# Eleven stretches of an attention kernel in another written order, and rows spread by GpSimd instead of by loads

## The chip, the cores and the metric

The kernel runs on one core of a Trainium2 chip. The metric is the device time of one execution in microseconds (us). A core has five engines that run at the same time, each through its own queue in the order in which its instructions are written: TensorE (PE; its weight loads are listed as PEld), VectorE (DVE), ScalarE (ACT), GpSimd (POOL) and SyncE (SP). SyncE only issues DMAs here: loads, and transposes of bf16 tiles. ScalarE and GpSimd issue a few DMAs too. All of them share 16 DMA engines.

## What is computed

Two blocks over the same 2048 rows of 640 numbers, multiplied at the end. Block A is attention of the normalized rows over the last 512 keys of a cache, 32 heads of 192, one key head for each query head. Block B picks the two rows with the largest dot product with a vector w_r, sends them through a gated feed-forward layer, and adds the result to those rows.

```
xn = layernorm(x)
q  = (xn @ wq) in 32 heads of 192
s  = softmax(q k^T / sqrt(192)) v, joined, @ wo        # k, v: last 512 of the cache
r  = xn @ w_r;  idx = the 2 rows with the largest r
y  = (silu(xn[idx] @ w_gate) * (xn[idx] @ w_up)) @ w_down * sigmoid(r[idx])
g  = silu(xn + y scattered to rows idx)
out = x + s * g
```

## The kernel before

**Tiling.** Rows lie in 16 blocks of 128. Heads come in pairs, and four heads make a group (8 groups). A *step* is one pair of heads for 512 rows; a *unit* is one pair for 128 rows, so there are 64 steps and 256 units. Units go through the engines in *stretches*: two of 2 units, then 84 of 3.

**A unit's way.** The letters are the tokens in which the order is written.

- `q.i.c` (L301): five matmuls project 512 rows for 128 of step i's 384 columns; `qe.i.c` scales the result out of PSUM on ScalarE (`a`) or VectorE (`v`), L291 and L293. With a row range at its end, a token is for half the rows; those evacuations go to ScalarE whatever their letter.
- `S.j` (L315, L322): scores of all units of a stretch, two PSUM tiles for a unit.
- `M.n.h` (L330): row maximum on VectorE. `E.n.h` (L337): exponential and row sum on ScalarE.
- `P.n` (L342): SyncE issues the DMA transpose of the exponentials.
- `O.n`, `OO.n.m` (L356): eight matmuls with v. `R.j` (L346) inverts the row sums; `Oe.n` (L371 or L369) scales the result on VectorE or ScalarE; `T.j` (L377) transposes a stretch's results by DMA.
- `W.w` (L404): twelve matmuls with wo for 128 rows and one group of heads; `We.w` copies or adds them into s_acc (L416, L418).

**Normalizing** stands at the front, among the first stretches. `bn` (L163, L165) takes statistics on VectorE, `as` (L233 to L235) by two ScalarE passes and a small GpSimd operation. 1 / deviation comes by `sq` and `rc` (square root on ScalarE, reciprocal on VectorE) or by `pw`, four GpSimd operations with a power of -0.5 (L211 to L214). `ap` (L249, L251) applies it. Blocks 0 to 3 are transposed by TensorE (`turn`, L258, L259), the others by DMA (`xT`, L262). The first k tile is transposed by TensorE too (`kt`, L273, L274).

**Loads**: `x`, `k`, `v`, `wq`, `wo` on SyncE, or on ScalarE with an `a` at the end; `kT` (L119) transposes a k tile by DMA. `B` tokens stand for work of block B, of which the first eleven stretches have none.

**Buffers.** PSUM has two tiles of kind f (q, and o of the `O` token) and six of kind p (scores, w, and o of `OO`). The exponentials have four buffers (`p_pool`), their transposes six, transposed q three.

**What sets the order.** The kernel turns Tile's scheduling off: each engine runs its instructions exactly as the tokens are written. The first eleven stretches, S.0 to S.10, are written by hand in the string FIRST; from S.11 on `stretch(j)` writes the same pattern each time, with projections and output projections dealt out by a small plan (2 or 3 `q`, 1 or 2 `W` a stretch); the last stretches are by hand again (LAST).

**Block B** runs beside it. `m_open` loads w_r to all partitions (L444). `m_top` finds candidates in each block and sends them through DRAM to all partitions (L489, L491), `m_sel` reads them (L497). `m_down` sends the feed-forward's two rows through DRAM to all partitions (L612, L614), and `m_add` adds them on GpSimd to the chosen rows (L618 to L622).

Of the kernel before, what the change touches and what calls it, by code (L numbers as in the profile page):

```python
# [12 lines left out]
FP32 = mybir.dt.float32  # L13
BF16 = mybir.dt.bfloat16
# [7 lines left out]
def kernel(ctx, tc, A_x, A_k_cache, A_v_cache, A_wq, A_wo, B_x, B_w_r, B_w_gate, B_w_up, B_w_down, out):  # L22
    nc = tc.nc
    P = 128
    _, S, D = A_x.shape
# [49 lines left out]
    def f_tile(shape, dtype, name):  # L75
        return ps_f.tile(shape, dtype, name=name, tag="f")
# [60 lines left out]
    for _ in range(10):  # L137
# [5 lines left out]
        out=ident_f, in_=ident_f, compare_op=ALU.not_equal, fill=1.0, base=0,  # L143
# [291 lines left out]
    M = {}  # L435

    def m_open():
        late.close()
        M["stack"] = ExitStack()
        M["w"] = M["stack"].enter_context(tc.tile_pool(name="moe_w", bufs=1))  # L440
        M["s"] = M["stack"].enter_context(tc.tile_pool(name="moe_s", bufs=1))
        M["ws"] = (M["w"], M["s"])
        M["wr"] = M["s"].tile([P, D], BF16, name="wr_bc", tag="t3")
        nc.gpsimd.dma_start(out=M["wr"], in_=B_w_r.partition_broadcast(P))  # L444
        M["r"] = M["s"].tile([P, NTB], FP32, name="r_pn")
        M["r_b"] = M["s"].tile([P, P], BF16, name="r_b", tag="turned")
# [12 lines left out]
        nc.gpsimd.iota(M["cpos"], pattern=[[1, NCD]], base=0, channel_multiplier=0, allow_small_or_imprecise_dtypes=True)
# [16 lines left out]
    def m_top():  # L476

        rows = M["s"].tile([NTB, P], FP32, name="r_rows", tag="rows")
        nc.vector.tensor_copy(out=rows, in_=M["rT"][0:NTB, :])
        top = M["s"].tile([NTB, 8], FP32, name="top8")  # L480
        loc = M["s"].tile([NTB, 8], U32, name="loc8")
        nc.vector.max(out=top, in_=rows)
        nc.vector.max_index(out=loc, in_max=top, in_values=rows)
        cand = M["s"].tile([NTB, 2, 2], FP32, name="cand")
        nc.vector.tensor_copy(out=cand[:, 0, :], in_=top[:, 0:2])
        nc.vector.tensor_copy(out=cand[:, 1, :], in_=loc[:, 0:2])
        nc.vector.tensor_scalar(out=cand[:, 1, :], in0=cand[:, 1, :], scalar1=M["base"][:, 0:1], scalar2=None, op0=ALU.add)  # L487
        c_d = tc.dram_tile([NTB, 2, 2], FP32, name="c_d")
        nc.gpsimd.dma_start(out=c_d, in_=cand)  # L489
        M["cand"] = M["w"].tile([P, NTB, 2, 2], FP32, name="cand_bc", tag="w")  # L490
        nc.gpsimd.dma_start(out=M["cand"].rearrange("p n k c -> p (n k c)"), in_=c_d.rearrange("n k c -> (n k c)").partition_broadcast(P))  # L491
# [108 lines left out]
    DQ = D // 4  # L600

    def m_down():
        y_ps = f_tile([P, DQ], FP32, "y_ps")
        for fc in range(FC):
            for c in range(4):
                nc.tensor.matmul(y_ps[32 * c:32 * c + 32], lhsT=M["hT"][:, fc, :], rhs=M["wd"][:, fc, c * DQ:(c + 1) * DQ],
                                 start=(fc == 0), stop=(fc == FC - 1), skip_group_check=True)
        y_sb = M["s"].tile([P, DQ], BF16, name="y_sb", tag="t2")
        nc.vector.tensor_scalar(out=y_sb, in0=y_ps, scalar1=M["sgp"][:, 0:1], scalar2=None, op0=ALU.mult)  # L609
        y_d = tc.dram_tile([2, D], BF16, name="y_d")  # L610
        for c in range(4):
            nc.gpsimd.dma_start(out=y_d[:, c * DQ:(c + 1) * DQ], in_=y_sb[32 * c:32 * c + 2, :])  # L612
        M["y_bc"] = M["w"].tile([P, 2, D], BF16, name="y_bc", tag="w")
        nc.gpsimd.dma_start(out=M["y_bc"], in_=y_d.partition_broadcast(P))  # L614

    def m_add(n):
        def f():
# [162 lines left out]
    for j in range(2, NST):  # L780
        due = sum(st_of[4 * i] <= j + 1 for i, _ in todo)
        k = max(due, 2) if j % 4 != 1 else max(due, 3)
# [3 lines left out]
        k = 2 if len(ready) >= 2 and len(q_in[j]) <= 2 and (done + 1) <= 1.5 * (j - 4) else 1  # L786
        k = {NST - 4: 1, NST - 3: 1, NST - 2: 3, NST - 1: 2}.get(j, k)
# [69 lines left out]

    for token in FIRST:
# [43 lines left out]
```

## Time and profile before

| | |
|---|---|
| three runs | 807.45, 809.00, 809.56 us (median 809.0) |
| the profiled execution | 808.71 us, its span 806.9 us |
| granted TensorE clock, mean of the span | 0.997 |
| PE busy | 785.0 us (97%), 5748 matmuls |
| DVE busy | 623.1 us (77%) |
| ACT busy | 480.5 us (60%) |
| POOL busy | 171.9 us (21%) |
| SyncE and ScalarE's main DMA queue, share of 16 engines | 93.3% |

The profile is of one execution. The span runs from the first to the last instruction; the execution's own time is 1.8 us longer. Lines such as L404 are lines of the kernel before; in the changed kernel every line from L447 on has a number two higher. In a group or timeline row, `out<-in` names the tiles written and read, and a bracket says how long the engine sat idle just before and what ended that. A row with SPq is a DMA issue on SyncE's queue: its length is how long the issue took, not the transfer.

### The profile page before, as it was taken

To read this page: it belongs to the slowest core of one execution; us is meant where nothing else is said; L and a number is where in the kernel's file an instruction comes from. 1 tells how busy PE (TensorE), PEld (TensorE's weight loads), DVE (VectorE), ACT (ScalarE), POOL (GpSimd) and SP (SyncE) were. 2 spreads that over 40 slices of the span, in tenths; PEclk is the share of its full clock that TensorE was granted. 3 is DMA by queue.
4 is the path that set the end of the run, shared out by engine and by line. 5 is a ranking of instruction groups with operands and counts; after the bars stand their busy time and mean duration, and the time that the engine had idled before them with its cause. 6 is when DMAs were issued, how large, how long until landed. Compare 5 with 4: busy or idle time off the path is not lost. (4 is left out here: it accounts for less than half of the span.)

```text
span 806.9 us, 15632 instructions
## 1 busy us (share of the span) xinstructions
PE 785.0 (97%) x5748; PEld 481.6 (60%) x5748; DVE 623.1 (77%) x1242; ACT 480.5 (60%) x1299; POOL 171.9 (21%) x187
## 2 busy tenths in 40 slices
PE   7799999999999999999999999999999999999996
PEld 3355555666566665666656665666665666566665
DVE  6775478989887777777777777777788888777786
ACT  5796666565556655665555565566556865565560
POOL 0330000000000000000001899920000000265954
PEclk9999999999999999999999999999999999999999
DMA  8999898799979999799997899869997899997994
GB/s 224 201 209 219 159 208 134 134 187 183 187 124 206 198 210 210 128 209 213 188 229 145 163 180 202 160 122 184 201 166 134 148 180 209 167 194 153 167 177 117
DMA packets 453389, 143.80 MB, mean 178 GB/s; under 512 B 422350, under 2 KB 452816, under 8 KB 453312
## 3 DMA queue, kind: packets, MB, share of 16 engines
q1 hardware_dynamic: 451712, 139.94, 93.3%
q0 software_dynamic: 928, 2.50, 1.1%
q8 instruction: 45, 0.74, 0.4%
q10 hardware_dynamic: 672, 0.36, 0.1%
q14 instruction: 32, 0.26, 0.1%
HBM read 39.98 MB, written 2.62 MB: 53 GB/s over the span
## 5 line engine op out<-in xcount | busy, mean ns | idle before, releaser
L337 ACT ACTIVATE pexp<-sc,nm 128x512 bf16<-128x512 f32 x512 | 348.0, 695 | 287.4 <-issue 241.8
L330 DVE TENSOR_REDUCE nm<-sc 128x1 f32<-128x512 f32 x512 | 315.0, 681 | 74.8 <-PE sc L322 74.8
L301 PE MATMUL q_ps<-xnT,wq_p 128*128 128x512 bf16 (+1 forms) x975 | 227.4, 379 | 7.5 <-DMA xnT<-xn 2.6
L404 PE MATMUL w_ps<-wo_g,oT 128*128 128x320 bf16 x1542 | 223.6, 299 | 0.8 <-DMA wo_g<-in_A_wo_dram 0.6
L404 PEld LDWEIGHTS <-oT 128*128 128x128 bf16 x1542 | 150.1, 98 | 72.0 <-issue 1.5
L356 PE MATMUL o_ps<-v_sb,pT 128*128 128x192 bf16 x2048 | 185.2, 246 | 4.4 <-DMA pT<-pexp 4.4
L356 PEld LDWEIGHTS <-pT 128*128 128x128 bf16 x2048 | 171.1, 98 | 18.2 <-DMA pT<-pexp 5.3
L371 DVE TENSOR_TENSOR o_sb<-o_ps,lsum 128x384 bf16<-128x384 f32 x245 | 134.9, 556 | 49.2 <-PE o_ps L356 31.0
L301 PEld LDWEIGHTS <-wq_p 128*128 128x128 bf16 x975 | 89.0, 98 | 132.8 <-issue 41.3
L315 PE MATMUL sc<-kT,qT 128*128 128x512 bf16 x512 | 125.4, 379 | 0.5 <-DVE o_sb L371 0.3
L418 DVE TENSOR_TENSOR s_acc<-s_acc,w_ps 128x320 f32<-128x320 f32 x192 | 92.1, 483 | 32.1 <-PE w_ps L404 32.1
L337 ACT ACTIVATION_READ_ACCUMULATOR pexp<-sc,nm 128x1 f32 x512 | 109.6, 214 | 0.0
L293 ACT ACTIVATE qT<-q_ps 128x512 bf16<-128x512 f32 (+1 forms) x184 | 101.5, 605 | 3.4 <-PE q_ps L301 3.2
L315 PEld LDWEIGHTS <-qT 128*128 128x128 bf16 x512 | 48.9, 98 | 41.7 <-issue 0.7
L322 PE MATMUL sc<-kT,qT 64*128 64x512 bf16 x512 | 70.3, 380 | 0.0
L643 POOL TENSOR_TENSOR s_acc<-s_acc,xn 128x640 f32<-128x640 f32 x16 | 22.4, 1401 | 114.1 <-DVE s_acc L418 114.1
L322 PEld LDWEIGHTS <-qT 64*128 64x128 bf16 x512 | 18.0, 94 | 47.0 <-issue 36.2
L622 POOL TENSOR_TENSOR xn<-xn,yh 128x640 bf16<-128x640 bf16 x32 | 44.6, 1393 | 2.7
L612 POOL DMA_DIRECT2D y_d<-y_sb x4 | 2.2, 551 | 172.5 <-DVE y_sb L609 172.5
L644 POOL TENSOR_TENSOR s_acc<-s_acc,x_fin 128x640 f32<-128x640 f32 x16 | 22.4, 1398 | 62.8 <-DMA x_fin<-in_A_x_dram 61.9
L489 POOL DMA_DIRECT2D c_d<-cand x1 | 0.6, 551 | 158.6 <-DVE cand L487 158.6
L621 POOL TENSOR_SCALAR yh<-y_bc,oh 128x640 bf16<-128x640 bf16 x32 | 25.6, 798 | 4.5 <-DMA y_bc<-y_d 2.9
(104 smaller groups left out, 222.8 us busy)
## 6 DMA issues: line engine op xcount, KB each, us to landing
wq_p<-in_A_wq_dram SPq DMA_DIRECT2D x16, 480.0 KB, 5.3
wo_g<-in_A_wo_dram SPq DMA_DIRECT2D x16, 480.0 KB, 4.5
v_sb<-in_A_v_cache_dram SPq DMA_DIRECT2D x16, 384.0 KB, 3.9
k_raw<-in_A_k_cache_dram SPq DMA_DIRECT2D x31, 192.0 KB, 3.3
pT<-pexp SPq DMA_TRANSPOSE x256, 3.7
x_fin<-in_A_x_dram SPq DMA_DIRECT2D x16, 160.0 KB, 2.8
x_in<-in_A_x_dram SPq DMA_DIRECT2D x6, 320.0 KB, 4.1
wgu<-in_B_w_gate_dram SPq DMA_DIRECT2D x15, 128.0 KB, 2.6
```

What stands on the lines that cost most here:

```text
L293: nc.scalar.activation(out=out, in_=in_, func=ACT.Copy, scale=scale)
L301: nc.tensor.matmul(q_ps, lhsT=wq_of[g * PAIRS + pr][:, dc, c * P:(c + 1) * P], rhs=xnT[:, t5 * 4 + lo:t5 * 4 + hi, dc, :], start=(dc == 0) ...
L315: nc.tensor.matmul(sc_of[n][hh], lhsT=qT_of[i][:, 2 * hh, u * P:(u + 1) * P], rhs=kp[:, :, 2 * hh, :], start=True, stop=False)
L322: nc.tensor.matmul(sc_of[n][hh], lhsT=qT_of[i][hs, 1, u * P:(u + 1) * P], rhs=kp[hs, :, 1, :], start=False, stop=True)
L330: nc.vector.tensor_reduce(out=nm_of[j][:, c:c + 1], in_=sc_of[n][hh], axis=AX.X, op=ALU.max, negate=True)
L337: nc.scalar.activation(out=pe_of[n][:, hh, :], in_=sc_of[n][hh], func=ACT.Exp, bias=nm_of[j][:, c:c + 1], scale=1.0, accum_out=l_of[j][:, ...
L356: nc.tensor.matmul(ps[:, hh, :], lhsT=pT_of[n][:, hh, jj, :], rhs=v_sb[:, hh, jj, :], start=(jj == 0), stop=(jj == NJ - 1))
L371: nc.vector.tensor_tensor(out=osb_of[j][:, m], in0=ps, in1=l_of[j][:, 2 * m:2 * m + 2].unsqueeze(2).to_broadcast([P, 2, Dh]), op=ALU.mult)
L404: nc.tensor.matmul(w_ps, lhsT=oT_of[j][:, stretches[j].index(n), c % 3, :], rhs=wo_of[g][:, c, lo:hi], start=(c == 0), stop=(c == CPG - 1))
L418: nc.vector.tensor_tensor(out=acc, in0=acc, in1=w_ps, op=ALU.add)
L621: nc.gpsimd.tensor_scalar(out=yh, in0=M["y_bc"][:, j, :], scalar1=M["oh"][:, n, j:j + 1], scalar2=0.0, op0=ALU.mult, op1=ALU.add)
L622: nc.gpsimd.tensor_tensor(out=xn[:, n, :], in0=xn[:, n, :], in1=yh, op=ALU.add)
```

## The change

In three places of block B a row goes to one partition first, and GpSimd's partition_broadcast copies it to all 128. The hand-written order FIRST is another one, for the same work: the same units, projections, output projections and loads lie in it. Tokens of one kind are served by other engines in places. Compared by count up to S.10: statistics by `as` 7 instead of 5 (`bn` pairs 9 instead of 11), `pw` groups 4 instead of 3 (blocks 2 and 3 by power, not by square root), `Oe` on ScalarE 17 instead of 11, `We` on ScalarE 3 instead of 7, full `qe` on ScalarE 9 instead of 14, loads issued by ScalarE 5 instead of 2. As built, GpSimd has two extra instructions without tile names at each broadcast (one ahead of it, and the broadcast itself), and one more ahead of the next ordinary instruction that follows (L457, L545 and L620 of the changed kernel).

```diff
         M["wr"] = M["s"].tile([P, D], BF16, name="wr_bc", tag="t3")
-        nc.gpsimd.dma_start(out=M["wr"], in_=B_w_r.partition_broadcast(P))
+        row = M["s"].tile([1, D], BF16, name="wr_row", tag="t1")
+        nc.gpsimd.dma_start(out=row, in_=B_w_r.rearrange("(o d) -> o d", o=1))
+        nc.gpsimd.partition_broadcast(M["wr"], row)
...
-        c_d = tc.dram_tile([NTB, 2, 2], FP32, name="c_d")
-        nc.gpsimd.dma_start(out=c_d, in_=cand)
+        row = M["s"].tile([1, NTB, 4], FP32, name="cand_row", tag="t2")
+        nc.gpsimd.dma_start(out=row, in_=cand.rearrange("n k c -> n (k c)"))
         M["cand"] = M["w"].tile([P, NTB, 2, 2], FP32, name="cand_bc", tag="w")
-        nc.gpsimd.dma_start(out=M["cand"].rearrange("p n k c -> p (n k c)"), in_=c_d.rearrange("n k c -> (n k c)").partition_broadcast(P))
+        nc.gpsimd.partition_broadcast(M["cand"].rearrange("p n k c -> p (n k c)"), row.rearrange("o n k -> o (n k)"))
...
-        y_d = tc.dram_tile([2, D], BF16, name="y_d")
+        row = M["s"].tile([1, 2, 4, DQ], BF16, name="y_row", tag="rows")
         for c in range(4):
-            nc.gpsimd.dma_start(out=y_d[:, c * DQ:(c + 1) * DQ], in_=y_sb[32 * c:32 * c + 2, :])
+            nc.gpsimd.dma_start(out=row[:, :, c, :], in_=y_sb[32 * c:32 * c + 2, :])
         M["y_bc"] = M["w"].tile([P, 2, D], BF16, name="y_bc", tag="w")
-        nc.gpsimd.dma_start(out=M["y_bc"], in_=y_d.partition_broadcast(P))
+        nc.gpsimd.partition_broadcast(M["y_bc"].rearrange("p k d -> p (k d)"), row.rearrange("o k c d -> o (k c d)"))
...
-x.0.2.3.a x.0.0.1 x.0.1.2 bn.0.0 bn.1.0 bn.0.1 bn.1.1 sq.0.1 sq.1.2 rc.0.1 k.0.0 rc.1.2 k.0.1 ap.0.v ap.1.v x.0.3.4 sx wq.0 kt.0.a x.1.0.2 kt.1.a turn.0.v turn.1.a x.1.2.4 q.0.0.0.2 q.0.2.0.2 B.2.0 bn.2.0 qe.0.0.v.0.2 q.0.1.0.2 qe.0.2.v.0.2 bn.3.0 qe.0.1.v.0.2 bn.2.1 wq.1 bn.3.1 sq.2.4 bn.7.0 ex rc.2.4 ap.3.v k.1.0 ap.2.v
- S.0 turn.3.a M.0.1 M.0.0 turn.2.a E.0.0 q.0.0.2.4 bn.7.1 q.0.2.2.4 k.1.1 M.1.0 qe.0.0.v.2.4 M.1.1 E.1.0 v.0 q.0.1.2.4 bn.6.0 kT.1 bn.6.1 qe.0.2.a.2.4 qe.0.1.v.2.4 as.5 bn.4.0 x.2.0.2 v.1 bn.4.1 E.1.1 E.0.1 P.1
- S.1 M.2.0 E.2.0 M.2.1 q.1.2 x.2.2.4 pw.4.8 E.2.1 qe.1.2.a bn.8.0 bn.8.1 P.2 q.1.0 M.3.0 M.3.1 qe.1.0.a ap.7.g ap.5.v q.1.1 B.3.3 ap.4.v E.3.0 ap.6.v E.3.1 P.0 xT.4.6 qe.1.1.a
- S.2 R.0 M.4.0 M.5.0 bn.11.0 O.1 as.9 O.0 M.4.1 bn.11.1 E.4.0 as.10 xT.6.8 M.5.1 M.6.0 pw.8.12 Oe.0.a E.4.1 E.5.0 Oe.1.a E.6.0 R.1 P.3 q.2.0 M.6.1 qe.2.0.v q.2.1 x.3.2.4 q.2.2 B.4.0 B.2.1 qe.2.1.v B.2.3 P.4 ap.11.v T.0 E.6.1 P.6 O.2 E.5.1 qe.2.2.v
...
- S.6 Oe.12.a M.17.0 ap.13.g xT.14.16 q.5.2 xT.12.14 M.16.0 M.18.0 M.17.1 v.2 E.17.0 P.15 B.8.0 E.16.0 qe.5.2.v M.16.1 wo.1.0 E.18.0 E.16.1 R.5 B.7.0 k.2.0.a B.5.2 W.2 M.18.1 E.18.1 q.6.0 E.17.1 B.8.3 B.5.0 qe.6.0.a B.4.2 k.2.1 W.1 We.1.v OO.13.14 Oe.13.v We.2.a wq.2 Oe.14.v P.16 O.15
...
- S.8 Oe.18.v B.9.1 M.22.0 E.22.0 k.3.0 M.23.0 wq.3 R.7 q.7.0 q.7.1 M.22.1 M.24.0 E.23.0 k.3.1 P.20 M.23.1 E.22.1 M.24.1 E.23.1 E.24.0 E.24.1 qe.7.1.v W.6 OO.19.20 P.22 W.5 We.5.a We.6.a qe.7.0.a Oe.19.v O.21 Oe.20.v
...
+B.3.3 x.0.0.1.a x.0.1.2 k.0.0 bn.0.0 k.0.1.a bn.1.0 x.0.2.3 bn.0.1 sx sq.0.1 wq.0 bn.1.1 sq.1.2 kt.0.a rc.0.1 ap.0.v rc.1.2 kt.1.v x.0.3.4 ap.1.v bn.2.0 turn.0.a turn.1.v q.0.0.0.2 q.0.2.0.2 ex bn.2.1 qe.0.0.v.0.2 k.1.0.a bn.3.0 bn.3.1 qe.0.2.v.0.2 wq.1.a x.1.2.4 q.0.1.0.2 qe.0.1.a.0.2 x.1.0.2 pw.2.4 
+S.0 k.1.1 as.4 ap.2.v ap.3.v turn.2.v turn.3.a M.0.0 q.0.0.2.4 E.0.0 M.1.0 q.0.2.2.4 qe.0.0.v.2.4 E.1.0 bn.7.0 q.0.1.2.4 M.0.1 qe.0.2.v.2.4 v.1 qe.0.1.a.2.4 bn.6.0 B.2.0 bn.7.1 E.0.1 
+S.1 bn.6.1 x.2.0.2 M.1.1 q.1.2 x.2.2.4 as.5 q.1.0 pw.4.8 v.0 M.2.1 E.1.1 qe.1.2.a M.2.0 E.2.0 R.0 M.3.1 E.2.1 as.8 q.1.1 ap.6.g ap.4.v ap.5.v M.3.0 B.3.2 E.3.0 qe.1.0.v P.0 kT.1 bn.11.0 B.3.1 bn.9.0 ap.7.v O.0 qe.1.1.v E.3.1 bn.11.1 P.1 
+S.2 B.3.0 P.2 B.2.1 bn.9.1 xT.4.6 xT.6.8 M.4.0 as.10 P.3 B.4.0 M.5.0 pw.8.12 Oe.0.a M.4.1 O.1 E.5.0 M.5.1 q.2.0 E.5.1 x.3.0.2 Oe.1.v E.4.0 M.6.0 E.6.0 qe.2.0.v T.0 x.3.2.4 E.4.1 P.4 q.2.1 R.1 q.2.2 M.6.1 qe.2.1.v B.2.2 ap.8.g qe.2.2.v E.6.1 ap.9.g O.2 
...
+S.6 q.5.1 M.16.0 E.16.0 B.4.1 xT.14.16 B.8.0 B.5.0 P.15 ap.13.g M.17.1 M.16.1 M.17.0 qe.5.1.a B.7.3 xT.12.14 E.16.1 k.2.0 q.5.2 M.18.0 B.4.2 M.18.1 W.2 R.5 E.17.0 wo.1.0 E.18.0 We.2.v E.17.1 k.2.1 B.7.1 P.16 OO.13.14 E.18.1 W.1 q.6.0 B.6.2 qe.5.2.v P.18 Oe.13.a Oe.14.a We.1.v O.15 T.4 P.17 
+S.7 Oe.15.v qe.6.0.v M.20.0 q.6.1 B.10.3 M.19.0 M.21.0 qe.6.1.v E.19.0 B.5.1 M.21.1 M.20.1 M.19.1 E.20.0 q.6.2 E.21.0 E.19.1 E.20.1 W.3 O.18 W.4 T.5 wq.2.a v.2 qe.6.2.v E.21.1 We.4.v OO.16.17 k.3.0 R.6 We.3.a Oe.16.v Oe.17.a 
+S.8 M.22.0 Oe.18.a M.23.1 E.22.0 B.9.1 P.21 M.22.1 q.7.0 R.7 M.24.1 P.19 M.23.0 P.20 E.22.1 E.23.0 B.7.0 q.7.1 qe.7.0.a k.3.1 qe.7.1.a E.23.1 W.6 M.24.0 W.5 We.6.v E.24.0 wq.3 E.24.1 OO.19.20 B.6.0 P.22 Oe.19.a T.6 We.5.v Oe.20.a B.9.0 
...
```

## Prediction, on record before the changed kernel ran

> **What bounds the kernel now.** I read the page's busy table and its slices first, to see which engine has no room.
>
> ```profile
> PE 785.0 (97%) x5748; PEld 481.6 (60%) x5748; DVE 623.1 (77%) x1242; ACT 480.5 (60%) x1299; POOL 171.9 (21%) x187
> PEclk9999999999999999999999999999999999999999
> DMA  8999898799979999799997899869997899997994
> ```
>
> TensorE is busy for 97% of the span, and the slices show the DMA engines near full from the start. Next the windows: they say where TensorE's missing 3% lies. The columns are the stretch, its length, busy time (and instructions) of PE, PEld, DVE, ACT and POOL, the granted clock, the DMA share and GB/s.
>
> ```profile
> 0.00:20.00 20.00, 15.19 (x89) 7.84 (x90) 12.82 (x38) 11.57 (x25) 0.73 (x7) 0.91 0.83 224
> 20.00:40.00 20.00, 15.62 (x95) 7.69 (x94) 14.52 (x31) 15.78 (x45) 6.24 (x13) 1.00 1.01 200
> 40.00:60.00 20.00, 19.21 (x141) 11.53 (x139) 16.24 (x34) 18.77 (x52) 6.64 (x19) 1.00 1.10 210
> 60.00:80.00 20.00, 18.11 (x131) 10.63 (x129) 11.52 (x22) 12.03 (x35) 0.00 (x0) 1.00 1.17 220
> 80.00:100.00 20.00, 18.41 (x132) 11.12 (x130) 10.38 (x20) 12.15 (x34) 0.00 (x0) 1.00 0.87 159
> 100.00:120.00 20.00, 20.00 (x149) 12.39 (x147) 14.03 (x28) 13.68 (x39) 0.00 (x0) 1.00 1.09 207
> ```
>
> From 100 us on TensorE is full up to the last 27 us (20.15 of them), and those the change does not touch. So time can be won or lost only in the first 110 us, which is just the part written anew, or by stopping TensorE later. What it waited for there, with total, times and longest wait:
>
> ```profile
> PE o_ps L356 <- DMA pT<-pexp: 3.6, 3, 1.7
> PE q_ps L301 <- DMA xnT<-xn: 2.6, 1, 2.6
> PE q_ps L301 <- DMA wq_p<-in_A_wq_dram: 1.8, 1, 1.8
> PE q_ps L301 <- ACT qT L293: 1.5, 1, 1.5
> PE q_ps L301 <- ACT xnT L259: 1.2, 1, 1.2
> PE w_ps L404 <- DMA wo_g<-in_A_wo_dram: 0.6, 1, 0.6
> ```
>
> **A ruler for TensorE.** The first score matmuls (L315) of stretches 0 to 11 start, in TensorE's timeline, at 12.83, 18.10, 24.67, 35.31, 43.48, 50.11, 60.01, 71.86, 81.69, 93.00, 102.00 and 111.66. Later the starts repeat: 7.92 where a stretch holds two projections q and one output projection W, 9.01 with a third q, 9.55 with a second W. So q costs 1.08 and W 1.63; what is left, 4.13, is scores of three units, 1.99 (0.66 a unit), and 24 matmuls of L356 in one row of 2.14 (0.71 a unit). Period less work is what TensorE lost: S.0 5.27 less 3.74 is 1.5; then S.1 2.0, S.2 3.3, S.3 0.1, S.4 0.3, S.5 0.9, S.6 2.3, S.7 0.3, S.8 1.8, S.9 0, S.10 0.1. **Together 12.6 us.** The new order does the same matmuls by S.11; it changes only these losses.
>
> **The new order, stretch by stretch.** I laid both written orders out queue by queue by the means of rows: exponential 0.66 from one start to the next, maximum 0.64, two-pass statistics on ScalarE 1.72, evacuation of q 0.59 on ScalarE and 0.67 on VectorE, transpose 1.25 of SyncE, pow group 2.0. The old order so laid out reaches S.11 at 111.3 (trace 111.66) and is off by 1.3 at most between, which is my error for one stretch.
>
> *Head.* The first weights wq.0 are issued fourth on SyncE (about 2.3) instead of sixth (3.69), ahead of one x load; before, they landed 5.9 after issue, at 9.6, and TensorE waited 1.8. But the copy of row block 1 now waits on VectorE behind the k copy: its statistics end at 6.1, 1 / deviation comes at 6.9, k copy 0.58, apply 0.44, transposes 0.4, copy 0.49 with three hand-overs end at about 9.4. So the first q starts at 9.1 to 9.6 against 9.66: I count 0. Two more loads issued by ScalarE (0.6 each) stand between evacuations that wait for TensorE anyway. Pow for blocks 2 and 3 takes 1.33 to its result (20.48 to 21.81 in the row of the first group); it starts at about 10.9, the two applies end by 13.1, and TensorE is in S.0 until 14.5: cover 1.4.
>
> *S.0: 1.6 (was 1.5).* ScalarE ends the last early evacuation at 13.5, then runs a statistics pair (to 15.2) and the copy of block 3 (to 15.8), from which three half q (1.6) and an evacuation lead to S.1 at about 18.1.
> *S.1: 1.9 (2.0).* Before, q.1.1 waited 1.5 for a PSUM buffer behind ScalarE's queue. Now that is 0.5, but O.0, drawn into this stretch, waits 1.4 for the buffer that VectorE empties after two maxima and two applies.
> *S.2: 2.5 (3.3).* Before, the transpose of blocks 6 and 7 was issued 2.7 after S.2 began and landed at 6.7; TensorE had 3.4 to do and waited 2.6. Now it is issued at 0.9 and lands 4.0 later, at 4.9; TensorE has 2.7 to do and waits 2.1, and 0.4 more on PSUM.
> *S.3 to S.5: 1.0 (1.3).* The wait for wo (0.6) goes, since both halves are issued a stretch earlier; short PSUM waits come instead (0.3 to 0.6 each).
> *S.6: 0.6 (2.3).* This is the clearest gain:
>
> ```profile
> 63.95 3.59 SPq L342 DMA_TRANSPOSE pT<-pexp  x1
> 71.19 0.34 PE L356 MATMUL o_ps<-v_sb,pT 128*128 128x192 bf16 x2 [1.69 <-DMA pT<-pexp]
> 83.80 3.49 SPq L342 DMA_TRANSPOSE pT<-pexp  x1
> ```
>
> The first row is unit 15's transpose. It stands right behind the v.2 load, takes 3.59 of SyncE's time instead of 1.25, and TensorE waits for it at 71.19. In the new order it stands ahead of every load of its stretch; v.2 moves to S.7. A PSUM wait of 0.5 stays.
> *S.7: 0.2 (0.3).*
> *S.8: 1.6 (1.8).* The third row is its cause before, behind two k and one wq. The new order has such a place too: unit 21's transpose behind v.2, k.3.0 and (ScalarE's queue) wq.2. At 3.5 to issue and 6.2 to landing it keeps one of four exponential buffers, ScalarE waits for that, and W.5 waits 1.6 for PSUM.
> *S.9, S.10: 0.2 (0.1).*
>
> The sum is 9.6 against 12.6: **3.0 gained**, and from S.11 on the rigid periods carry it to the end. Work shifts between ScalarE (about 1 more) and VectorE (about 2.4 more) over 100 us; neither is full there.
>
> **The broadcasts.** No row shows GpSimd's broadcast. Nearest for one is a one-input pass of 640 elements, 0.80, and of 1280, twice that; the dearest is two passes of 1.40. Each comes with code to be fetched, and the next ordinary instruction with another. The bound below is L142, which has such an instruction ahead of it and starts 0.9 after GpSimd's last; above, a 480 KB load, 5.9 to 7.8. What hides it: the weights row is needed at 134.1, and GpSimd is free from 57; y's 16 row blocks end at 530, and the first reader is at 582. The tightest is the candidates:
>
> ```profile
> 218.23 0.55 POOL L489 DMA_DIRECT2D c_d<-cand  x1 [158.60 <-DVE cand L487]
> 221.65 0.59 POOL L491 DMA_DIRECT2D cand_bc<-c_d  x1 [2.87 <-PE sc L322]
> 235.00 0.17 DVE L497 COPY val<-cand_bc 128x32 f32<-128x32 f32 x1
> ```
>
> Now they land at 226.2. With the gather (0.55 and 2.9) beside a fetch of 7.8 from 218.8, and 0.8 for the broadcast, it is 227.4, still 7.6 early. Cost 0; without cover, the loads it replaces would save at most the 4.5 of one landing, which nobody waits for. The Trainium skill, GPSIMD Engine Reference, section 2.1 Instruction dispatch, speaks against the change: the first call of a freshly loaded kernel pays about 6 us that the profile does not name. An estimate by it: six switches are 36 us of GpSimd, the candidates come at 225.6, and the sum is the same.
>
> **Sum.** The profiled execution took 808.7 (span 806.9); 3.0 less is 805.7. The runs' median, 809.0, lies 0.3 above it, so I say 806.0. About 0.3% (2.4 us) is what a measurement can tell here.
>
> **Rivals.**
> *The order gives back most of it (808.0).* In S.1 the transposes of unit 0 and of kT.1 stand behind v.0. If they are held as at 63.95 (2.3 more), kT.1 (issued at about 20, landing 3.8 later, needed at 24.9) makes S.2 1.2 late, and the 0.8 of S.2 goes: 1.0 is left. Against: transposes soon after x loads (23.09) took 1.23.
> *Slower (812.0): transposes behind loads.* Four more groups of the new order have loads just ahead of a transpose (wo.0 before unit 10, k.2 and wo.1 before 16, k.3 and wq.3 before 22, v.3 before 28). The two that hurt before cost 2.3 and 1.8. At 2.0 each on top of my 806.0, one group gives 808.0, two 810.0, and from the third on (812.0) it is slower by more than the bound, 811.4. For it: DMA shares above 1.00 in 20 to 80. Against: laid out, new transposes land 1.5 or more ahead of their readers, in the old order 0 to 1.
> *GpSimd late (slower).* From 16.8 us after the candidates are ready, VectorE waits, SyncE behind it (its wgu load needs the same buffer), and each further us costs one: at 20 us the gain of 3.0 is undone, from 22 on it is slower.
> *The clock (804.5).* The granted clock was 0.50 from 9.57 to 12.98, and 15 half q took 3.38 there against 1.88 at 16.38. If that window falls otherwise, 1.5 more is gained. The Trainium skill, TensorE: Matmul & The Clock Gate, Part 1, says that the gate judges free-running windows of 3413 ns; the 3.41 seen here agrees.
>
> **Chances.** My forecast 0.52 (804 to 808; 0.42 of it beyond the bound at 806.6, 0.10 within), clock 0.10, giving back 0.24, loads 0.10, GpSimd 0.04. So faster 0.52, same 0.34, slower 0.14. The range, 802.8 to 809.8, takes in all but the slower cases and the far end of the clock's.
>
> **What will show it.** Right: S.11 at about 108.7, no wait for pT near S.6, the xnT wait nearer 2, periods after S.11 unchanged, candidates read without a wait. Wrong: transposes of 3.5 on SyncE followed by waits of TensorE for pT or of ScalarE for a buffer; kT among TensorE's waits; VectorE idle at its copy of the candidates.

## The result, and the profile after

The changed kernel took 804.26 us (median of six runs, 802.13 to 805.80), the kernel before 808.13 beside it (six runs, 807.40 to 809.56): a ratio of 0.9954, with a 95% interval from 0.9937 to 0.9971. The profiled execution after took 803.71 us, its span 801.8, so 5.0 less than the profiled execution before.

First the page's busy table and clock and DMA slices, as before:

```profile
PE 786.1 (98%) x5748; PEld 482.0 (60%) x5748; DVE 624.9 (78%) x1243; ACT 481.9 (60%) x1303; POOL 176.0 (22%) x195
PEclk9999999999999999999999999999999999999998
DMA  7999998799969999699997999878997899997994
```

The work is the same; GpSimd has 8 rows more. Now the windows of the stretches that were written anew (columns as in the prediction: stretch, length, busy time of PE, PEld, DVE, ACT, POOL, granted clock, DMA share, GB/s):

```profile
0.00:20.00 20.00, 15.69 (x93) 8.11 (x94) 12.74 (x37) 12.67 (x28) 2.26 (x12) 0.91 0.76 226
20.00:40.00 20.00, 17.23 (x96) 8.09 (x95) 16.38 (x34) 17.36 (x49) 7.29 (x15) 0.91 1.10 198
40.00:60.00 20.00, 19.82 (x146) 11.34 (x144) 16.48 (x33) 17.29 (x49) 5.31 (x10) 1.00 1.06 210
60.00:80.00 20.00, 19.05 (x140) 12.11 (x139) 13.49 (x26) 11.54 (x34) 1.92 (x10) 1.00 1.08 217
80.00:100.00 20.00, 20.00 (x143) 11.72 (x142) 12.95 (x25) 13.45 (x38) 0.00 (x0) 1.00 1.24 203
```

TensorE is full from 80 us on (before: from 100). But the clock is 0.91 in the second window too, where it was 1.00: this execution met two stretches of half clock, the one before met one. What TensorE waited for in 0 to 110, the five longest in total:

```profile
PE q_ps L301 <- DMA xnT<-xn: 1.6, 2, 0.9
PE warm_ps L138 <- DVE idle L135: 1.2, 1, 1.2
PE o_ps L356 <- DVE qT L291: 1.0, 1, 1.0
PE tp_k L273 <- DMA k_raw<-in_A_k_cache_dram: 0.9, 1, 0.9
PE sc L315 <- DMA kT<-k_raw: 0.9, 1, 0.9
```

The 3.6 us of waits for pT are gone, and so are those for wq and wo; a wait for kT has come. With the prediction's ruler (a stretch's period less its work):

| lost by TensorE, us | S.0 | S.1 | S.2 | S.3 to S.5 | S.6 | S.7 | S.8 | S.9, S.10 | sum |
|---|---|---|---|---|---|---|---|---|---|
| before | 1.5 | 2.0 | 3.3 | 1.3 | 2.3 | 0.3 | 1.8 | 0.1 | 12.6 |
| forecast | 1.6 | 1.9 | 2.5 | 1.0 | 0.6 | 0.2 | 1.6 | 0.2 | 9.6 |
| measured | 1.0 | 2.9 | 2.5 | 0.8 | 1.1 | 0.0 | 0.1 | 0.1 | 8.5 |

S.11 starts at 107.35, 4.3 us sooner (4.1 less is lost, and S.0 starts 0.2 sooner). From S.11 to S.85 it is 667.7 us against 668.5, another 0.8: before, a wait for pT of 0.7 fell into S.44.

GpSimd's broadcasts, from its timeline (start, length, instruction, idle time before it):

```profile
62.80 0.62 POOL L446 PARTITION_BROADCAST wr_bc<-wr_row  x1 [5.67 <-issue]
...
71.69 0.14 POOL L457 IOTA iota<- 128x16 f32 x1 [7.04 <-issue]
...
213.75 0.71 POOL L491 DMA_DIRECT2D cand_row<-cand  x1 [141.71 <-DVE cand L489]
220.37 0.37 POOL L493 PARTITION_BROADCAST cand_bc<-cand_row  x1 [5.91 <-PE w_ps L404]
...
439.74 0.93 POOL L616 PARTITION_BROADCAST y_bc<-y_row  x1 [5.89 <-PE w_ps L404]
...
447.56 0.72 POOL L620 TENSOR_SCALAR xn<-xn 128x640 bf16<-128x640 bf16 x1 [6.88 <-issue]
```

A broadcast takes 0.37 to 0.93 us. Ahead of each GpSimd idles 5.7 to 5.9, though its row had landed over 3 us before, and 6.9 to 7.0 ahead of the IOTA and the TENSOR_SCALAR of L620 that follow. The Trainium skill, GPSIMD Engine Reference, 2.1 Instruction dispatch, gives about 6 us for the first call of a freshly loaded kernel; the trace agrees with 5.7 to 5.9, and shows the way back at 7. Over all nine traces with broadcasts it is 5.7 to 6.6 ahead of one and 6.9 to 9.9 on the way back. The candidates are there at 220.7 and are read at 230.5, without a wait.

### The profile page after: what moved, and what is told of

Same layout as the page of the kernel before. It is cut to its first block, busy times and chain, and to the rows that moved or that the text cites. A ratio compares the mean times of both kernels' runs of the same rounds, so it can differ in the third digit from the quotient of the medians.

```text
span 801.8 us, 15662 instructions
## 1 busy us (share of the span) xinstructions
PE 786.1 (98%) x5748; PEld 482.0 (60%) x5748; DVE 624.9 (78%) x1243; ACT 481.9 (60%) x1303; POOL 176.0 (22%) x195
## 3 DMA queue, kind: packets, MB, share of 16 engines
q10 hardware_dynamic: 2512, 1.54, 0.7%
## 4 chain that ended last, share of the span: by engine, by line
PE 70%; DVE 2%; DMA 1%; ACT 1%; issue 0%; DVEq 0%; ACTq 0%
PE w_ps L404 20%; PE q_ps L301 18%; PE o_ps L356 16%; PE sc L315 10%; PE sc L322 6%; DVE nm L330 1%; DMA pT<-pexp 1%; ACT pexp L337 1%; DVE xn L632 1%; ACT qT L293 0%; PE gu_ps L571 0%; DVE fin_t L423 0%; DVE fin_o L425 0%; PE y_ps L608 0%; PE tp_o L389 0%
## 5 line engine op out<-in xcount | busy, mean ns | idle before, releaser
L371 DVE TENSOR_TENSOR o_sb<-o_ps,lsum 128x384 bf16<-128x384 f32 x239 | 131.6, 557 | 40.3 <-PE o_ps L356 22.0
L293 ACT ACTIVATE qT<-q_ps 128x512 bf16<-128x512 f32 (+1 forms) x179 | 98.8, 606 | 2.5 <-PE q_ps L301 2.3
L614 POOL DMA_DIRECT2D y_row<-y_sb x4 | 2.3, 574 | 172.0 <-DVE y_sb L611 172.0
```

Of the source, the lines that this page charges most:

```text
L293: nc.scalar.activation(out=out, in_=in_, func=ACT.Copy, scale=scale)
L371: nc.vector.tensor_tensor(out=osb_of[j][:, m], in0=ps, in1=l_of[j][:, 2 * m:2 * m + 2].unsqueeze(2).to_broadcast([P, 2, Dh]), op=ALU.mult)
```

## The experiments

My theory after the two traces: **the written order carries the gain, the broadcasts nothing**; 1 us of it lies in the head (up to S.5) and 3 in S.6 to S.10, where transposes no longer stand behind loads. The rivals: the removed loads gave a part; the DMA engines are full, so a wait taken away comes back elsewhere; the clock, not the order, made the difference between the traces.

Each run was timed in five rounds beside the kernel before. A ratio's interval is some 0.2% to each side (1.6 us), so the start of S.6 and S.11 in the profiled execution is the finer measure, though of one execution each. All results side by side ("half clock" counts stretches of 3.41 us at a granted clock of 0.50: H one that began before 20 us, 2 one that began from 26 to 33 us, mostly in S.2; new_fill is a case of its own, told under The clock; S.0, S.6 and S.11 are starts; in the new head q.5.1, 1.1 us, is moved from S.5 to S.6, so the losses compare the heads, not S.6 alone):

| run | ratio to before, 95% | half clock | S.0 | S.6 | S.11 | lost S.0-5 | S.6+7 | S.8 | S.9+10 | S.11 to S.85 |
|---|---|---|---|---|---|---|---|---|---|---|
| before | 1 | H | 12.83 | 60.01 | 111.66 | 8.1 | 2.6 | 1.8 | 0.1 | 668.5 |
| after | 0.9954 (0.9937, 0.9971) | H, 2 | 12.62 | 57.80 | 107.35 | 7.3 | 1.2 | 0.1 | 0.1 | 667.7 |
| bc_only | 0.9987 (0.9970, 1.0004) | 2 | 11.22 | 60.05 | 110.87 | 9.8 | 2.1 | 1.4 | 0.1 | 667.5 |
| order_only | 0.9948 (0.9929, 0.9968) | 2 | 10.84 | 57.48 | 108.13 | 8.7 | 0.5 | 0.4 | 1.5 | 667.8 |
| head_new | 0.9979 (0.9958, 1.0000) | none | 11.33 | 56.12 | 108.69 | 6.9 | 2.9 | 1.3 | 0.1 | 668.6 |
| head_old | 0.9958 (0.9943, 0.9973) | none | 11.58 | 59.96 | 107.81 | 9.3 | 0.5 | 0.1 | 0.1 | 669.0 |
| old_p15 | 1.0000 (0.9983, 1.0018) | 2, 2 | 11.21 | 61.38 | 112.37 | 11.1 | 2.2 | 1.5 | 0.1 | 669.1 |
| new_p15_late | 0.9931 (0.9910, 0.9952) | none | 10.84 | 55.66 | 105.77 | 6.9 | 0.4 | 1.0 | 0.5 | 667.3 |
| new_kt_early | 0.9936 (0.9911, 0.9960) | H | 12.39 | 57.22 | 105.88 | 6.9 | 0.0 | 0.1 | 0.3 | 668.0 |
| new_sqrt | 0.9966 (0.9952, 0.9980) | H, 2 | 10.74 | 60.17 | 110.54 | 11.5 | 0.3 | 0.3 | 1.5 | 668.1 |
| old_p20 | 0.9975 (0.9961, 0.9989) | 2 | 11.31 | 61.13 | 110.70 | 10.8 | 2.3 | 0.0 | 0.1 | 666.7 |
| new_fill | 0.9935 (0.9916, 0.9955) | up to 10.3 | 12.04 | 56.60 | 107.08 | 6.7 | 0.0 | 1.3 | 0.9 | 668.0 |
| old_fill | 1.0023 (1.0009, 1.0038) | none | 11.16 | 58.99 | 109.19 | 8.8 | 2.1 | 0.8 | 0.1 | 670.7 |
| new_xt_early | 0.9940 (0.9916, 0.9964) | 2 | 10.95 | 56.56 | 105.23 | 7.5 | 0.0 | 0.1 | 0.3 | 668.6 |

### The two parts of the change, each alone

**bc_only**: the changed kernel with the string FIRST of the kernel before.

> The three broadcasts alone, in the written order of the kernel before. My theory: nothing, since every row that GpSimd spreads is read long after it is there. Time within 1 us of before (ratio 0.999 to 1.001), S.11 at 111.7, the candidates ready near 225 and read at 235 without a wait. Rival A (the loads were what cost): 128 copies of a row leave the queues, and S.6 and S.11 start 0.7 to 1.5 us sooner. Rival B (GpSimd's code): its operations in the head come late, and S.6 starts 1 us later or more.

**order_only**: the kernel before with the new FIRST.

> The new written order alone, rows still spread by loads. My theory: it carries the whole gain, ratio near 0.995, S.11 at 107.3 to 107.6 (before 111.66) and the same losses of TensorE as in the changed kernel (S.1 2.9, S.2 2.5, S.6 1.1, S.8 0.1). Rival: part of the gain came from the loads that the broadcasts removed; then S.11 starts at 108.1 or later.

The order alone gave 0.9948, the whole change 0.9954, the broadcasts alone 0.9987 with 1 in its interval. So the order carries the gain. The broadcasts cannot be told from nothing; up to 2.4 us (0.3%) is not excluded, and bc_only's S.11 at 110.87 instead of 111.66 does not decide it, as the next runs show how far one execution strays. The candidates were there before they were read (233.7, no wait). Order_only's S.11 came at 108.13, in the rival's range, but by waits in S.10 (0.7 and 0.4) that new_sqrt, with broadcasts, shows as well; so it does not speak for the loads.

### The two halves of the order, each alone

**head_new**: the new order to S.5, the old one after it (with q.5.1 added there). **head_old**: the other way round.

> The new order up to S.5, the old one from S.6 to S.10, broadcasts by GpSimd. My theory: the parts add up. Of the 4.3 us, the head gave 1.05 and S.6 to S.10 3.3; so S.11 at about 110.6 and 1.1 us less than before (ratio near 0.9987), with the wait for pT in S.6 (1.7) and the loss in S.8 (1.8) back. Rival: the gain in S.6 to S.10 depends on the head's end, and S.11 comes out below 109.5 or above 111.5.

> The old order up to S.5, the new one from S.6 to S.10, broadcasts by GpSimd. My theory: S.11 at about 108.4 and 3.3 us less than before (ratio near 0.996); TensorE's losses 8.1 up to S.5 as before, 1.2 from S.6 on. Rival: without the new head the waits of S.6 and S.8 stay in part, and S.11 starts at 109.5 or later.

Both misses are plain in the traces: S.11 at 108.69 (I said 110.6) and 107.81 (108.4). The two traces that I had read the split from had not met the same clock, and neither of these met half clock at all. Start of S.0 plus what is lost up to S.6, at like clock (runs with a token moved in the head or with idle matmuls counted in): without half clock 19.9 and 20.9 with the old head, 17.8 and 18.2 with the new one; with one stretch of it 21.0, 21.0 and 22.1 against 18.5, 18.7, 19.3 and 19.6; with two 22.3 against 19.9 (new_sqrt left out). So the new head is worth 2.3 to 2.4 by the means, from values up to 1.1 apart, not the 1.05 that the traces of before and after show, since after met one half-clock stretch more. Some of it is given back by S.11: in the old order S.6 to S.10 lose 4.2 behind the new head and 3.7 by the mean of four behind the old one, in the new order 1.4 by the mean of six and 0.7. In the medians the parts add up: against bc_only's 0.13%, the head gave 0.08% more and S.6 to S.10 0.29%, 0.50% in all against 0.46% measured together. That would be 0.6 us for the head; an interval of 0.2% on each leaves both splits possible.

### The clearest gain of the prediction: unit 15's transpose behind v.2

**old_p15** moves it ahead of the load in the old order; **new_p15_late** puts it behind that load in the new one.

```diff
- S.6 ... M.17.1 v.2 E.17.0 P.15 B.8.0 ...
+ S.6 ... M.17.1 P.15 v.2 E.17.0 B.8.0 ...
```

> The kernel before with one token moved: in S.6 the transpose of unit 15 is issued ahead of the v.2 load instead of behind it. My theory: the transpose issues in about 1.3 to 1.6 instead of 3.59 and TensorE's wait of 1.69 at 71.19 goes; S.7 starts 1.5 to 1.7 sooner (70.2) and so does S.11 (110.0), ratio near 0.998. Rival: the DMA engines are full there, so that the wait stays in another place (v.2 late, or another transpose behind it): S.11 within 0.4 of 111.66.

```diff
-S.6 ... B.5.0 P.15 ap.13.g M.17.1 M.16.1 M.17.0 qe.5.1.a B.7.3 xT.12.14 E.16.1 ...
+S.6 ... B.5.0 ap.13.g M.17.1 M.16.1 M.17.0 qe.5.1.a B.7.3 xT.12.14 v.2 P.15 E.16.1 ...
-S.7 ... wq.2.a v.2 qe.6.2.v ...
+S.7 ... wq.2.a qe.6.2.v ...
```

> The changed kernel with v.2 moved back from S.7 into S.6 and the transpose of unit 15 put right behind it. My theory: the transpose issues in 3 us or more and TensorE waits for pT at O.15, so that S.11 starts 1 to 2 us later than in the changed kernel (108.4 to 109.3 against 107.35). Rival: O.15 stands at the end of S.6 in the new order and the transpose still lands in time; S.11 within 0.3 of 107.35.

Both theories fell. S.11 (112.37 and 105.77) lies outside the rivals' ranges too, but the first rival named what came: the wait moved to another place. In old_p15 the issue is short and the wait for pT is gone, but the two xT just ahead landed late, and TensorE waited for those. SyncE's and then TensorE's row:

```profile
64.69 1.39 SPq L342 DMA_TRANSPOSE pT<-pexp  x1
```
```profile
68.20 1.25 PE L301 MATMUL q_ps<-xnT,wq_p 128*128 128x512 bf16 x5 [1.45 <-DMA xnT<-xn]
```

In new_p15_late the transpose stands right behind v.2 (first row), takes 1.90, and TensorE lost nothing in S.6:

```profile
60.22 0.75 SPq L124 DMA_DIRECT2D v_sb<-in_A_v_cache_dram  x1
61.08 1.90 SPq L342 DMA_TRANSPOSE pT<-pexp  x1
```

And bc_only, which has the old tokens unchanged, issued it in 1.23:

```profile
62.99 0.67 SPq L124 DMA_DIRECT2D v_sb<-in_A_v_cache_dram  x1
63.76 1.23 SPq L342 DMA_TRANSPOSE pT<-pexp  x1
```

The same two tokens stand in head_new, old_fill and old_p20, which issued it in 1.23 or 1.24. So the 3.59 and the wait of 1.69 were one execution's. What does hold over executions is the sum of S.6 and S.7: 2.1 to 2.9 lost in each of the six traces with the old order there, 0.0 to 1.2 in each of the eight with the new one. Which tokens make it is not shown; TensorE's wait moved between pT, xnT and PSUM. One row of SyncE does differ throughout: unit 16's transpose, behind wo.1.0, k.2.1 and wq.2 in the old order and behind k.2.0, wo.1.0 and k.2.1 in the new one, took 2.2 to 5.0 in the six and 1.3 to 2.6 in the eight. No run moves it alone.

### The step of S.8: unit 20's transpose behind three loads

```diff
- S.7 ... W.4 P.19 We.4.a P.21
- S.8 ... k.3.0 M.23.0 wq.3 ... k.3.1 P.20 M.23.1 ...
+ S.7 ... W.4 P.19 We.4.a P.20 P.21
+ S.8 ... k.3.0 M.23.0 wq.3 ... k.3.1 M.23.1 ...
```

> The kernel before with the transpose of unit 20 issued at the end of S.7, ahead of unit 21's and of the three loads k.3.0, wq.3 and k.3.1, instead of behind them. Theory: this is the step of S.8; the issue takes 1.3 to 1.6 instead of 3.49 (2.8 to 3.5 in the four runs of the old order), TensorE's wait for pT (1.1 to 1.6 in those four) goes, S.8 takes 9.6 to 9.8 instead of 11.0 to 11.3, and 1.2 to 1.5 us are gained up to S.11. Rival: as with unit 15 another transfer is late in its place, and S.8 still takes 11 or more.

This one held in S.8. TensorE's rows of OO.19.20, before and in old_p20:

```profile
87.63 0.82 PE L356 MATMUL o_ps<-v_sb,pT 128*128 128x192 bf16 x8
90.04 0.83 PE L356 MATMUL o_ps<-v_sb,pT 128*128 128x192 bf16 x8 [1.59 <-DMA pT<-pexp]
```
```profile
88.43 1.48 PE L356 MATMUL o_ps<-v_sb,pT 128*128 128x192 bf16 x16
```

Ahead of the loads three transposes (units 19, 20, 21) issue in 4.06, 1.35 each; the loads follow:

```profile
79.76 4.06 SPq L342 DMA_TRANSPOSE pT<-pexp  x3
83.87 0.86 SPq L115 DMA_DIRECT2D k_raw<-in_A_k_cache_dram  x1
84.82 0.57 SPq L110 DMA_DIRECT2D wq_p<-in_A_wq_dram  x1
85.45 1.16 SPq L115 DMA_DIRECT2D k_raw<-in_A_k_cache_dram  x1
```

S.8 took 9.56 instead of 10.3 to 11.3 in the five others, which issued unit 20's transpose in 2.2 to 3.5 and waited 0.6 to 1.6 for it; here TensorE waited for no pT in S.8. S.11 came only 1.0 sooner than before, since S.0 to S.5 lost 2.7 more in this execution. In the timed rounds this single token gave 2.0 us (0.9975; 0.9 to 3.2): about half of what the whole change gave, by the medians. The new order has the like in it: units 21, 19 and 20 issue together, at 78.04, ahead of k.3.1 and wq.3.

### kT earlier, and then xnT

**new_kt_early** moves kT.1 from behind P.0 in S.1 to S.0.

```diff
-S.0 ... bn.6.0 B.2.0 bn.7.1 E.0.1
-S.1 ... qe.1.0.v P.0 kT.1 bn.11.0 ...
+S.0 ... bn.6.0 kT.1 bn.7.1 E.0.1
+S.1 ... qe.1.0.v P.0 bn.11.0 ...
```

> The changed kernel with the transpose of the second k tile (kT.1) issued in S.0, ahead of unit 0's transpose, instead of behind it in S.1. TensorE waited 0.91 for kT at the start of S.2. Theory A: that wait goes and S.3 starts 0.5 to 0.9 sooner (34.0), S.11 near 106.7. Theory B: q.2.0 waits for xnT, which lands at about 30.8 whatever TensorE does; S.3 within 0.3 of 34.73. Theory C: with less idle time between 22.9 and 26.3 the half-clock window at 26.3 to 29.75 does not come, and S.3 starts up to 2.3 sooner.

The wait for kT (0.8 to 0.95 in all five traces with kT.1 behind P.0) went: S.1 lost 1.8 instead of 2.8 to 3.0. The whole of it came back at q.2.0 (theory B); S.1 and S.2 together lost 5.6, and 5.3 to 5.5 with kT late where no half clock fell on q.2.0:

```profile
24.24 1.24 PE L315 MATMUL sc<-kT,qT 128*128 128x512 bf16 x5
30.70 1.67 PE L301 MATMUL q_ps<-xnT,wq_p 128*128 128x512 bf16 x7 [3.15 <-DMA xnT<-xn]
```

**new_xt_early** goes after that wait.

```diff
-S.1 ... E.2.1 as.8 q.1.1 ap.6.g ap.4.v ... P.0 bn.11.0 B.3.1 bn.9.0 ap.7.v O.0 ...
-S.2 B.3.0 P.2 B.2.1 bn.9.1 xT.4.6 xT.6.8 M.4.0 ...
+S.1 ... E.2.1 q.1.1 ap.6.g as.8 ap.4.v ... P.0 ap.7.v bn.11.0 B.3.1 bn.9.0 O.0 ...
+S.2 B.3.0 xT.4.6 P.2 xT.6.8 B.2.1 bn.9.1 M.4.0 ...
```

> The run new_kt_early with the chain to xnT moved up: block 6 is applied on GpSimd ahead of its part of the next statistics, block 7 on VectorE ahead of two bn passes, and SyncE issues both xT transposes ahead of unit 2's. In new_kt_early the second xT was issued at about 26.5, landed 4.1 later, and TensorE waited 3.15 at q.2.0. Theory: the second xT issues at about 24.1 and lands near 28.2, just when the PSUM buffer comes free (27.9); the wait falls under 1, S.2 loses 1.0 to 1.6 instead of 2.5 to 3.75, S.6 begins at 54.3 to 55.8 and S.11 at 104 to 105.3; the median comes 1 to 2 us under that of new_kt_early (ratio 0.991 to 0.993). Rival: unit 2's transpose, now behind two others, lands late, or later DMA waits take the gain back by S.11 (105.5 or later, ratio 0.9935).

As built, only the first xT stood ahead of unit 2's transpose (the expectation says both), and that is what it shows:

```profile
21.18 1.42 SPq L262 DMA_TRANSPOSE xnT<-xn  x1
22.70 2.45 SPq L342 DMA_TRANSPOSE pT<-pexp  x1
25.26 1.34 SPq L262 DMA_TRANSPOSE xnT<-xn  x1
```

Unit 2's issue took 2.45, the second xT went out at 25.26 and TensorE still waited 2.8, until 28.86; a half-clock stretch from 28.05 slowed q.2.0 on top, so that S.2 lost 4.3. S.11 at 105.23 is the earliest of all traces, but the ratio, 0.9940, can't be told from the changed kernel's. Both xT ahead of it was not tried.

### Power instead of square root

```diff
-... turn.1.v q.0.0.0.2 q.0.2.0.2 ex bn.2.1 ... x.1.0.2 pw.2.4
+... turn.1.v q.0.0.0.2 q.0.2.0.2 bn.2.1 ... x.1.0.2 sq.2.4 ex rc.2.4
```

> The changed kernel with 1 / deviation of blocks 2 and 3 by square root and reciprocal again, the exponential's table loaded behind it, as before. My theory: the power was covered, so its change is worth nothing: S.1 within 0.3 of 17.38. Rival: a load of the exponential's table (1.28) comes back into ScalarE's queue just ahead of the first stretch, and S.1 and S.11 start 0.7 to 1.5 later.

The load and the wait of the rival came; S.1, at 18.57, is 1.2 later, in its range, S.11, at 110.54, 3.2 later and beyond it. ScalarE's row of the table load, and TensorE's of the half projections that wait for block 3's copy behind it:

```profile
11.62 1.28 ACT L241 ACT_TABLE_LOAD   x1
```
```profile
15.42 3.36 PE L301 MATMUL q_ps<-xnT,wq_p 128*128 128x256 bf16 x15 [2.27 <-ACT xnT L259]
```

In order_only, with S.0 at nearly the same time, these start at 13.85 and wait 0.8. S.0 lost 4.1 instead of 1.0: 1.6 by the later copy (the load is 1.28 of it), 1.45 by half clock (3.36 against 1.91), which came just there. In the timed rounds it is 0.9966 against 0.9954, so 1 us, inside the intervals: in the time it isn't told from nothing.

### The clock

Half clock showed up in nine of the fourteen traces, for 3.41 us each time (in old_p15 twice in a row). The windows of that length, laid out from where each began, show what stood ahead of it (after, then bc_only, then new_kt_early; the third column from the end is the clock):

```profile
5.77:9.18 3.41, 1.57 (x22) 1.23 (x22) 2.21 (x8) 2.37 (x4) 0.00 (x0) 0.99 1.05 350
9.18:12.59 3.41, 3.07 (x15) 2.22 (x16) 2.19 (x8) 1.57 (x4) 1.22 (x4) 0.51 0.72 224
...
22.88:26.29 3.41, 1.56 (x12) 1.05 (x12) 3.38 (x9) 3.38 (x9) 1.07 (x2) 0.99 1.20 146
26.29:29.70 3.41, 3.41 (x16) 1.15 (x15) 1.97 (x5) 1.95 (x7) 1.94 (x6) 0.51 1.19 221
```
```profile
26.66:30.07 3.41, 0.83 (x8) 0.61 (x8) 2.88 (x7) 3.38 (x11) 1.72 (x5) 1.00 1.12 204
30.07:33.48 3.41, 3.23 (x8) 1.19 (x9) 0.69 (x1) 2.73 (x10) 1.82 (x3) 0.54 1.02 221
```
```profile
28.97:32.38 3.41, 1.69 (x8) 0.81 (x9) 1.42 (x3) 2.77 (x8) 1.93 (x3) 1.00 1.06 217
```

Ahead of each half-clock stretch lay such a window at full clock with PE busy for 0.67 to 1.57 us. None with 1.69 or more was followed by half clock, but neither were windows with 1.49 (new_p15_late), 1.54 (head_old) and 1.64 (head_new), so there is no sharp edge. (The windows are laid out right to 0.3 us; where one is off, its clock reads 0.51 or 0.54.) So I filled TensorE's waits with matmuls of zeros whose sums the next real matmul overwrites.

```diff
         q_ps = f_tile([P, (hi - lo) * P], FP32, "q_ps")
+        for _ in range(FILL.get((i, c, lo), 0)):
+            nc.tensor.matmul(q_ps, lhsT=idle[:, 0:P], rhs=idle[:, 0:(hi - lo) * P], start=True, stop=True)
```

(and six transposes of zeros ahead of the second turn in new_fill.)

> The changed kernel with kT.1 early (as in the run new_kt_early) and idle matmuls of zeros ahead of the second turn (6), the first q (4) and q.2.0 (12), in PSUM tiles that the next real matmul overwrites. In the traces so far the granted clock fell to 0.50 for 3.41 us after each such window in which TensorE was busy for 1.57 us or less, and where such a window falls is chance: one, two or none before 36 us. Theory A (the clock is the scatter): no half-clock window in any head, S.0 near 10.9, S.6 near 55.4, S.11 at 104.5 to 105.3, and the median 1 to 2 us under that of new_kt_early (ratio 0.990 to 0.992). Theory B (the DMAs set the pace, the clock is covered): S.6 at 56.5 or later without any half-clock window, ratio near 0.994.

> The kernel before with the same idle matmuls ahead of the first q (12) and q.2.0 (9). No half-clock window in the head. In the old order S.6 began at 60.0 with a half-clock window at 9.57, with one at 30.07 and with none, because TensorE waited longer for blocks 6 and 7 (q.2.0) and for wo (W.0). Theory A: S.6 at 59.9 to 60.1 again and nothing gained in the median (ratio 0.998 to 1.001): the old order cannot use the faster clock, the new one can. Theory B: S.6 and S.11 come 1 us or more sooner, and part of what the change gained in its trace is the clock's.

The rows of new_fill at q.2.0, with the idle matmuls in the place of the wait:

```profile
27.59 2.75 PE L305 MATMUL q_ps<-idle 128*128 128x512 bf16 x11 [0.29 <-ACT o_sb L375]
30.18 1.03 PE L307 MATMUL q_ps<-xnT,wq_p 128*128 128x512 bf16 x4
```

Neither trace has a half-clock stretch behind the start, but new_fill's TensorE came to full rate late. Five transposes took 0.74 there and four idle matmuls 1.04; in new_p15_late five took 0.44, in old_fill twelve such idle matmuls 1.47:

```profile
7.71 0.74 PE L262 MATMUL tp<-ident,xn 128*128 128x128 bf16 x5
9.44 1.04 PE L305 MATMUL q_ps<-idle 128*128 128x256 bf16 x4
```

The clock's record in that trace begins only at 10.33 (at 4.2 to 6.5 in the others), so its column doesn't show it. S.0 started at 12.04 instead of the 10.9 expected. S.6 at 56.60 is theory B's mark, but with the slow start this trace does not test theory A.

Neither kernel got faster: new_fill 0.9935 as new_kt_early 0.9936, old_fill 1.0023. New_fill's six runs still lie between 800.2 and 805.2, at a mean clock of 0.997 to 0.999. The clock of every timed run is on record: over the 216 of them, each set of runs of one kernel about its own mean, a run is 0.5 us longer for each 0.001 of mean clock less, and that goes with a third of the scatter (correlation -0.58). Which of the two makes the other isn't shown, since a wait of TensorE comes ahead of half clock too. But the changed kernel's six had 0.993 to 0.998 (median 0.9945), the kernel before 0.995 to 0.996 in the medians of its four sets: what the change gained is not the clock's. Nor did the median gain the 1 to 2 us of theory A, as far as intervals of 0.2% tell. In old_fill's trace S.11 came 2.5 us sooner than before (theory B's mark) and the end only 0.3: S.11 to S.85 took 670.7 instead of 668.5, with waits of TensorE for the evacuation of q (1.3 in all), pT (0.9) and PSUM (0.6), where the kernel before has 0.3, 0.7 and 0.3. Why it is slower in the timed rounds stays open.

No version was told from the changed kernel: the lowest ratios, 0.9931 to 0.9936, have intervals that overlap its own.

## Why the prediction came out right, and where it was wrong

The time (804.26 for 806.0, in the range) and the sign were right, and the order carries the gain as argued. The time is nearest to the rival of the clock (804.5), but the changed kernel's runs had no higher clock than those before. That the losses came within 1.1 us of the forecast (8.5 for 9.6) is in part luck: errors of both signs cancel in the sum.

- **Broadcasts, 0:** right as far as the runs can tell. A broadcast took 0.37 to 0.93, mostly under the 0.8 to 2.8 said. The idle time taken for a fetch was 5.7 to 7.0 in this trace, within 0.9 to 7.8; in other traces the way back took up to 9.9, above the bound, and no wait for it shows. The candidates came at 220.7 (227.4), 7.0 behind the gather's issue instead of 9.2.
- **S.6, 1.7 gained by unit 15's place:** the amount for S.6 and S.7 together, 1.8, was near (1.4 in the two traces; 2.1 to 2.9 against 0.0 to 1.2 over all). The mechanism fell: the same token behind the same load issued in 1.23 elsewhere, and moving it changed nothing in either order. I took one execution's wait for the order's. What S.6 still lost in this trace was a wait of 0.95 for xnT, not the 0.5 for PSUM of the forecast.
- **S.8, 1.6 (was 1.8):** mis-sized, and the largest miss in time, 1.5 us. The cause before was rightly named, and old_p20 shows it. But unit 21's transpose, which I expected to take 3.5 behind three loads in the new order, took 1.26:

```profile
78.04 1.26 SPq L342 DMA_TRANSPOSE pT<-pexp  x1
```

  Two of these loads were issued at 75.2 and 75.8, more than 2 us ahead; whether that gap matters wasn't tried. Nor is it the order's own: over the eight traces with it, this transpose took 1.3 in seven and 2.3 in one, but unit 19's, right behind, took 1.7 here and 3.0 to 4.0 in three others. W.5's wait for PSUM, 1.6 in the forecast, did come in two (0.8 and 1.1), and S.8 lost 1.0 and 1.3 there. So the place is there, and the 1.6 lies beyond the most that any of the eight lost.
- **S.1, 1.9:** measured 2.9. This is the rival that gives back: kT.1, behind v.0 and P.0 on SyncE, came 0.8 to 0.95 late where it said 1.2, in every trace of this head as written. It cost nothing in the end, because q.2.0 waits for xnT anyway (new_kt_early).
- **Head, 1.1 gained to S.6:** 1.05 in the two traces, but 2.3 to 2.4 at like clock.
- **S.0, 1.6:** measured 1.0 in every trace but new_sqrt's. **Up to S.0, 0:** right, 0.2. **Pow covered, 0:** the cover held, but the table load that it takes off ScalarE's queue, 1.6 in new_sqrt's trace, was never priced.
- **S.2 2.5:** the number is luck. I said a wait of 2.1 for xnT; TensorE waited 0.69 here, and half clock from 26.2 to 29.6 stretched its matmuls over most of the rest. In head_new, without half clock, 2.6 was lost with a wait of 2.38, which is the mechanism as forecast.
- **S.3 to S.5 1.0, S.7 0.2, S.9 and S.10 0.2:** near what was measured in this execution (0.8, 0.0 and 0.1). S.9 and S.10 lost 1.5 in two others.
- **Slower, transposes behind loads; GpSimd late:** neither came; of the four groups named, units 16 and 22 issued in 1.5 and 1.7. **The clock:** a window did fall otherwise, but one more came, not one less; four later traces met none, and idle matmuls didn't move the median.
- **Rigid periods after S.11:** right to 1 us only. The same 74 stretches took 666.7 to 670.7.

## What to carry to other kernels

A wait of 1 to 2 us for a DMA in one profile is a draw until a second execution of the same order shows it: take a second profile before a gain is built on it, and sum neighbouring stretches, which are steadier than the wait's name. Unit 20's transpose behind three loads was held, and waited for, in every execution that had it there, and moving that one token ahead of the loads gave about half of what the whole rewriting did. Loads ahead don't hold every transpose: unit 16's took 1.3 to 2.6 behind three loads in the new order. After a wait is taken away, look for the next transfer that the same engine needs; with old_p15 and new_kt_early it was late by about as much, with old_p20 none was.

## What the runs showed of the hardware beyond what I expected

- **Half clock without an idle window.** The Trainium skill, TensorE: Matmul & The Clock Gate, Part 1, has TensorE fall to half rate after an idle window of about 3.4 us. Here the length agrees (3.41), the condition does not: windows in which it was busy for 0.67 (old_p20) to 1.57 of 3.41 us (20 to 46%) came ahead of it, with no single wait over 2.8, while the longest wait of all (3.15, in new_kt_early) fell into two windows of 1.9 and 1.7 and brought none.
- **A transpose's issue varies with what is ahead of it.** On SyncE it took mostly 1.2 to 1.4 us, up to 2.45 right behind other transposes (unit 2's in new_xt_early), and 1.2 to 5.0 behind loads (5.0 is unit 16's in head_new); for the same token behind the same loads 1.23 in one execution and 3.59 in another.
- **GpSimd pays both ways**: over nine traces it idled 5.7 to 6.6 us before a broadcast and 6.9 to 9.9 before the next ordinary instruction, IOTA or the TENSOR_SCALAR of L620. The third way back, L545, is covered by a wait for VectorE.
